# Attention backward on one NeuronCore: score and dP matmuls on four 32-row strips of the array

## The chip, the cores and the metric

The kernel runs on one core of one Trainium2 chip. TensorE (PE in the profile, with PEld for its weight loads) multiplies on an array of 128 rows by 128 columns and writes to PSUM; VectorE (DVE), ScalarE (ACT) and GpSimd (POOL) do the elementwise work; SyncE (SP) issues most DMAs, POOL issues others. The metric is the device time of one execution in microseconds. Three runs of the kernel before took 2552.87 to 2571.11 us, median 2569.79.

A matmul here contracts over the partitions (rows) of its two operands: a stationary one, loaded into the array, and a moving one, whose columns (up to 512) stream through. Where a matmul uses only some rows of the array, its operands lie on the same partitions, and that range of partitions chooses the part of the array.

## The reference

One transformer block with adaptive layer norm, forward and backward. S = 2048 tokens, D = 512, 32 heads of 16 channels, everything handed over in bfloat16. The forward pass returns the output, the backward pass the gradients of the input, the weights and the conditioning vector.

```
h = layernorm(x) * (1 + ca) + sa
x = x + ga * attention(h)          # 32 heads, softmax(q k^T / 4) v, then wo
h = layernorm(x) * (1 + cb) + sb
x = x + gb * mlp(h)                # relu(h w1 + b1)^2 w2 + b2
out, vjp = jax.vjp(f, x, wqkv, wo, w1, b1, w2, b2, c, w_mod);  grads = vjp(grad_out)
```

What the change touches is the attention part of the backward pass. For each head, with P the unnormalised exponentials: scores = q k^T, P = exp(scores / 4), dP = dO v^T minus a term for each query row, dS = P * dP; then dV = P^T dO, dK = dS^T q, dQ = dS k. The kernel folds the normalisation into dO beforehand, and the row term into two extra channels: dO^T has 18 rows a head (16 channels and the row term in two bfloat16 parts), V^T has 18 (16 channels and two rows of ones), so that dP comes out of one matmul over 18 rows. Scores contract over 16 rows.

## The kernel before

The program has three parts: the forward pass with the MLP's backward woven in, the weight gradients of the MLP (`gen_dw1`, `gen_dw2`, from about 1060 to 1179 us), and the attention backward (`attn_bwd`, from 1179 to 2438 us), followed by the projections' gradients (`phase6`).

**Heads and groups.** Four heads form a group g, eight groups in all. In the transposed tensors in DRAM (QTq_d, KTq_d, VTq_d, dOTq_d) each group is 128 partitions by 2048 tokens, and head j of the group takes the 16 or 18 rows from partition 32 j on. For V^T and dO^T the heads are shifted by two places: head j lies from partition 32 ((j + 2) mod 4). The rows between are padding.

**The loop of `attn_bwd`.** For each group, each pair of heads jp (heads 2 jp and 2 jp + 1 of the group), each key chunk c of 512 keys, and each block ib of 128 queries there is one unit: 8 x 2 x 4 x 16 = 1024 units. For each head a of the pair, a unit has a score matmul (L1555, stationary Q^T block, moving K^T chunk, into PSUM tile st), an exponential (ScalarE, L1559, into pu), a dP matmul of the unit before it (L1494, stationary dO^T block, moving V^T chunk, into PSUM tile dp) and VectorE's product of dp and pu into ds (L1496). Every second unit PE also does eight matmuls into acckv (L1448, 16 columns of weights, 512 columns of data, two units' worth), and in the others sixteen into accq (L1470, two units' worth, with 16 columns of data). ds is transposed for accq mostly by DMA, four units at a time; one in eight of its blocks is transposed on PE (L1513) and copied by ScalarE (L1514). st and dp have three PSUM buffers each.

**Masked copies.** A score matmul uses the 64 rows of its pair (partitions 64 jp to 64 jp + 63), a dP matmul the other 64. Both heads' rows of Q^T and dO^T lie there, so the moving operand must be zero on the other head's rows: `self.masked` holds for each of the four heads of a group its own copy of K^T and V^T, each 128 partitions by 2048, in two tiles m01 and m23. They are set to zero once by eight memsets on VectorE (L1375, in `open_bwd`, which is called inside the weight-gradient stage), and after that only the head's own 16 or 18 rows are loaded (`pair_pieces`, L1414).

**Order of the work.** PE's and SyncE's order is that of the program text in all of this; POOL's too from `phase5` on. In the weight-gradient stage VectorE, ScalarE and POOL are still ordered by the scheduler. The loads for the next pair of heads are issued on POOL, spread over the units (L1544), each behind a one-element copy (L1543) that waits for a product of VectorE. m01 is used again at the end: `xhat1_6`, loaded in the last pair, is its first half.

Of the kernel before, what the change touches and what calls it, by code (L numbers as in the profile page):

```python
# [9 lines left out]
BF16 = mybir.dt.bfloat16  # L10
# [9 lines left out]
P = 128  # L20
DH = 16
# [84 lines left out]
class K:  # L106
# [1249 lines left out]
    def open_bwd(self):  # L1356

        nc = self.nc
        S, ST, D, DT = self.S, self.ST, self.D, self.DT
        self.open_pool("pad_r", bufs=1, side="right").tile([P, 240], BF16, name="pad_r")  # L1360
        xp = self.open_pool("p5x", bufs=1, side="right")
        self.wp = self.open_pool("p5w", bufs=1, side="right")
        cp = self.open_pool("p5c", bufs=1, side="right")
        m01 = xp.tile([P, 4 * S], BF16, name="m01")
        self.q0 = xp.tile([P, 2 * S + 3 * ST * 4 * DH], BF16, name="q0")
        self.xhat1_6 = m01[:, :ST * D].rearrange("p (st d) -> p st d", d=D)
        self.wq_6 = self.q0[:, :3 * DT * D].rearrange("p (kt n) -> p kt n", n=3 * D)
        nc.vector.memset(self.kvs[0:64], self.scale)
        nc.vector.memset(self.kvs[64:P], 1.0)
        m23 = cp.tile([P, 4 * S], BF16, name="m23")  # L1370
        self.masked = {n: [m[:, (2 * t + a) * S:(2 * t + a + 1) * S] for m in (m01, m23) for a in range(2)]
                       for t, n in enumerate(("KT", "VT"))}
        for ms in self.masked.values():
            for m in ms:
                nc.vector.memset(m, 0.0)  # L1375
        self.qp = self.open_pool("p5q", bufs=1, side="right")
        self.Tq = {}

# [35 lines left out]
    def pair_pieces(self, g, jp):  # L1414
        pieces = []
        for n, src, sh, rows in (("KT", self.KTq_d, 0, DH), ("VT", self.VTq_d, 2, DH + 2)):
            for j in (2 * jp, 2 * jp + 1):
                r = 32 * ((j + sh) % 4)
                pieces.append((self.masked[n][j][r:r + rows, :], src[g, r:r + rows, :]))
        return pieces  # L1420

    def attn_bwd(self):
# [7 lines left out]
        tc, nc = self.tc, self.nc  # L1430
# [5 lines left out]
        acckv = accp.tile([P, 512], F32, name="acckv")  # L1436
        nc.vector.memset(acckv[:], 0.0)
        accq = accp.tile([P, ST, 2, DH], F32, name="accq")
        masked, kvs = self.masked, self.kvs
        pend, pendq = [], []  # L1440

        def kv(u):
# [46 lines left out]
        def dP(u, a):  # L1489

            (T, g, jp, c, ib, kvT, pu, dsg, i, grp) = u
            rd = slice(64 - 64 * jp, 128 - 64 * jp)
            dp = dpp.tile([P, 512], F32, name="dp")
            nc.tensor.matmul(dp[:], lhsT=T["dOT"][rd, ib * P:(ib + 1) * P],  # L1494
                             rhs=masked["VT"][2 * jp + a][rd, 512 * c:512 * (c + 1)], start=True, stop=True)
            nc.vector.tensor_tensor(dsg[:, i, a], dp[:], pu[:, a, :], ALU.mult)  # L1496

        def dS(u):
# [19 lines left out]
        T = self.T0  # L1518
        turnq, last = [], None
        for g in range(NQ):  # L1520
            for jp in range(2):
# [15 lines left out]
                for c in range(SC):  # L1537
                    c0 = 512 * c
                    for ib0 in range(0, ST, G):
# [6 lines left out]
                        for i in range(G):  # L1546
# [4 lines left out]
                            pu = self.pup.tile([P, 2, 512], BF16, name="pu")  # L1551
                            for a in range(2):
                                stt = stp.tile([P, 512], F32, name="st")
                                rs = slice(64 * jp, 64 * jp + 64)
                                nc.tensor.matmul(stt[:], lhsT=T["QT"][rs, q], rhs=masked["KT"][2 * jp + a][rs, c0:c0 + 512],  # L1555
                                                 start=True, stop=True)
                                if last:
                                    dP(last, a)
                                nc.scalar.activation(pu[:, a, :], stt[:], ACT.Exp, scale=self.scale)  # L1559
# [351 lines left out]
```

The softmax here doesn't subtract the row's maximum and nothing guards it: scores larger than these inputs give would overflow.

## Time and profile before

| | |
|---|---|
| median of three runs | 2569.79 us (2552.87 to 2571.11) |
| span of the profiled execution | 2562.0 us |
| its own time outside the span | not given by the profile |
| PE busy | 2483.2 us, 97% |
| ScalarE busy | 2314.2 us, 90% |
| VectorE busy | 1767.4 us, 69% |
| POOL busy | 569.5 us, 22% |
| mean granted TensorE clock | 0.994 |
| L1496, product of dp and pu, 2048 times | 1236.2 us busy, 13.1 us idle before |
| L1559, exponential, 2048 times | 1073.7 us busy, 46.4 us idle before |
| L1555, score matmul, 2048 times | 638.4 us busy, mean 381 to 382 ns |
| L1494, dP matmul, 2048 times | 690.3 us busy, mean 381 to 382 ns |

How to read it: the page's first lines give the busy time of each engine and its share of the span, then the span in 40 slices. A matmul's line has rows and columns of the array (64*128: 64 rows, 128 columns) and the shape of its operand. Matmuls overlap in the pipeline, so the mean length of one is longer than the time between two starts. A group's busy time counts overlapping instructions once; "idle before" is the time in which the engine stood still just before them, with what ended it. In the tables of stretches each line has the stretch, its length, then busy time and number of instructions for PE, PEld, DVE, ACT and POOL, then the granted clock as a share of full speed, the DMA share and GB/s. In the chain of work each line has start, length and what the end of the program hung on in that time.

### The profile page before, as it was taken

To read this page: it belongs to the slowest core of one execution; us is meant where nothing else is said; L and a number is where in the kernel's file an instruction comes from. 1 tells how busy PE (TensorE), PEld (TensorE's weight loads), DVE (VectorE), ACT (ScalarE), POOL (GpSimd) and SP (SyncE) were. 2 spreads that over 40 slices of the span, in tenths; PEclk is the share of its full clock that TensorE was granted. 3 is DMA by queue.
4 is the path that set the end of the run, shared out by engine and by line. 5 is a ranking of instruction groups with operands and counts; after the bars stand their busy time and mean duration, and the time that the engine had idled before them with its cause. 6 is when DMAs were issued, how large, how long until landed. Compare 5 with 4: busy or idle time off the path is not lost.

```text
span 2562.0 us, 77852 instructions
## 1 busy us (share of the span) xinstructions
PE 2483.2 (97%) x31239; PEld 1227.4 (48%) x31239; DVE 1767.4 (69%) x3651; ACT 2314.2 (90%) x3757; POOL 569.5 (22%) x1137
## 2 busy tenths in 40 slices
PE   8999899999999999899999999999999999999998
PEld 4555555555555554663444444444444444444443
DVE  6222323323322344667999999999999999999957
ACT  7999999999999996436999999999999999999935
POOL 3554521320221131353011111111111111111223
PEclk9999999999999999999999999999999999999999
DMA  4588742450351153799999999999999999999997
GB/s 165 118 180 196 173 95 83 100 113 22 112 128 49 39 143 113 154 190 211 205 205 202 199 200 201 203 204 200 197 199 198 208 201 197 201 201 229 213 202 191
DMA packets 1193040, 425.37 MB, mean 166 GB/s; under 512 B 1138004, under 2 KB 1161686, under 8 KB 1192678
## 3 DMA queue, kind: packets, MB, share of 16 engines
q1 hardware_dynamic: 1153542, 319.25, 64.2%
q0 software_dynamic: 37056, 100.11, 13.1%
q8 instruction: 244, 4.00, 0.6%
q10 hardware_dynamic: 2080, 1.05, 0.1%
q14 instruction: 118, 0.97, 0.1%
HBM read 73.73 MB, written 62.40 MB: 53 GB/s over the span
## 4 chain that ended last, share of the span: by engine, by line
PE 67%; ACT 20%; DMA 5%; issue 4%; POOL 2%; DVE 1%; SPq 1%; POOLq 0%; DVEq 0%; ACTq 0%
PE st L1555 20%; ACT pu L391 16%; PE acckv L1448 11%; PE accq L1470 8%; PE st L388 7%; PE accbank L322 3%; PE dp L1494 3%; ACT pu L1559 2%; PE st L1513 2%; PE dps L1047 2%; PE pps L1234 2%; PE dp L1604 1%; PE st L1699 1%; DMA dsT<-ds 1%; DMA ev_tm<-ev_fm 1%
## 5 line engine op out<-in xcount | busy, mean ns | idle before, releaser
L1496 DVE TENSOR_TENSOR ds<-dp,pu 128x512 bf16<-128x512 f32 x2048 | 1236.2, 679 | 13.1 <-PE dp L1494 10.2
L1559 ACT ACTIVATE pu<-st 128x512 bf16<-128x512 f32 x2048 | 1073.7, 612 | 46.4 <-PE dp L1494 22.5
L391 ACT ACTIVATE pu<-st 128x1024 bf16<-128x1024 f32 x992 | 912.1, 1077 | 4.6 <-PE st L388 4.4
L388 PE MATMUL st<-QTm,KTq 128*128 128x512 bf16 x1984 | 588.6, 377 | 19.5 <-ACT pu L391 6.0
L322 PEld LDWEIGHTS <-pu 128*128 128x128 bf16 x8192 | 347.5, 96 | 236.1 <-issue 3.1
L322 PE MATMUL accbank<-Vaug,pu 128*128 128x17 bf16 x8192 | 357.7, 171 | 1.2 <-ACT Vaug L522 0.9
L1494 PE MATMUL dp<-m,q 64*128 64x512 bf16 x1024 | 345.7, 382 | 1.1 <-DVE g2w L1053 0.7
L1494 PE MATMUL dp<-m,dOTg 64*128 64x512 bf16 x1024 | 344.6, 381 | 0.1
L1470 PEld LDWEIGHTS <-dsT 128*128 128x128 bf16 x8192 | 239.5, 96 | 213.8 <-issue 209.7
L1555 PE MATMUL st<-m,q 64*128 64x512 bf16 x1024 | 319.5, 382 | 9.2 <-ACT pu L1559 7.5
L1555 PE MATMUL st<-m,QTg 64*128 64x512 bf16 x1024 | 318.9, 381 | 9.5 <-ACT pu L1559 7.8
L388 PEld LDWEIGHTS <-KTq 128*128 128x128 bf16 x1984 | 188.3, 96 | 176.9 <-issue 125.5
L1543 POOL COPY tick<-ds 1x1 bf16<-1x1 bf16 x223 | 39.6, 178 | 1005.4 <-DVE ds L1496 1005.4
L1448 PE MATMUL acckv<-ds,q 128*16 128x512 bf16 x1024 | 154.0, 381 | 0.0
L1448 PE MATMUL acckv<-pu,dOg 128*16 128x512 bf16 x1024 | 154.0, 381 | 0.0
L1448 PE MATMUL acckv<-ds,Qg 128*16 128x512 bf16 x1024 | 154.0, 381 | 0.0
L1448 PE MATMUL acckv<-pu,q 128*16 128x512 bf16 x1024 | 154.0, 381 | 0.0
L1514 ACT COPY dsT<-st 128x512 bf16<-128x512 bf16 x256 | 152.4, 595 | 1.0 <-PE st L1513 1.0
L1470 PE MATMUL accq<-Kg,dsT 128*128 128x16 bf16 x4096 | 143.3, 170 | 3.4 <-DMA dsT<-ds 3.4
L1470 PE MATMUL accq<-q,dsT 128*128 128x16 bf16 x4096 | 143.6, 170 | 0.4 <-DMA dsT<-ds 0.3
L302 POOL DMA_DIRECT2D QTm<-QTq_d x124 | 63.3, 512 | 341.3 <-PE st L388 320.2
L329 DVE RECIPROCAL rl<-accbank 128x4 f32<-128x4 f32 x128 | 22.9, 179 | 162.6 <-PE accbank L322 162.5
(379 smaller groups left out, 2864.8 us busy)
## 6 DMA issues: line engine op xcount, KB each, us to landing
KTq<-KTq_d POOLq DMA_DIRECT2D x24, 512.0 KB, 3.9
duT_d<-auT POOLq DMA_DIRECT2D x3, 1792.0 KB, 7.8
aT_d<-rT POOLq DMA_DIRECT2D x3, 1792.0 KB, 11.1
KTq_d<-KTq SPq DMA_DIRECT2D x32, 128.0 KB, 2.0
QTq_d<-ev_fm SPq DMA_DIRECT2D x32, 128.0 KB, 3.9
VTq_d<-vT POOLq DMA_DIRECT2D x4, 1024.0 KB, 6.8
dsT<-ds SPq DMA_TRANSPOSE x256, 6.7
dx<-dx_d SPq DMA_DIRECT2D x16, 256.0 KB, 4.4
```

Source lines behind the costliest of these rows:

```text
L302: nc.gpsimd.dma_start(QTm[j][32 * j:32 * j + 32, :], self.QTq_d[g, 32 * j:32 * j + 32, 512 * qc:512 * (qc + 1)])
L322: nc.tensor.matmul(acc[:, a, sub, :], lhsT=pu[:, a, sub * P:(sub + 1) * P], rhs=Vaug[:, kb, h, :], start=(kb == 0 and a == 0 and sub == 0) ...
L388: nc.tensor.matmul(stt[:, a, :], lhsT=KT[:, kb * P:(kb + 1) * P], rhs=QTm[2 * jp + a][:], start=True, stop=True)
L391: nc.scalar.activation(pu[:], stt[:], ACT.Exp, scale=self.scale)
L1047: nc.tensor.matmul(pt[:], lhsT=a[st], rhs=g_tm[:, st, :], start=(st == 0), stop=(st == ST - 1))
L1448: nc.tensor.matmul(acckv[r:r + DH, :], lhsT=T[n][:, ib, col:col + DH], rhs=src[:, a, :], start=(ib == 0), stop=(ib == ST - 1))
L1470: nc.tensor.matmul(accq[:, ib, a, :], lhsT=dsT[:, (i * 2 + a) * 4 + sub, :], rhs=T["K"][:, 4 * c + sub, col:col + DH], start=(c == 0 and i ...
L1494: nc.tensor.matmul(dp[:], lhsT=T["dOT"][rd, ib * P:(ib + 1) * P], rhs=masked["VT"][2 * jp + a][rd, 512 * c:512 * (c + 1)], start=True, sto ...
L1496: nc.vector.tensor_tensor(dsg[:, i, a], dp[:], pu[:, a, :], ALU.mult)
L1514: nc.scalar.copy(dsT[:, 0:4, :], tp[:])
L1555: nc.tensor.matmul(stt[:], lhsT=T["QT"][rs, q], rhs=masked["KT"][2 * jp + a][rs, c0:c0 + 512], start=True, stop=True)
L1559: nc.scalar.activation(pu[:, a, :], stt[:], ACT.Exp, scale=self.scale)
```

## The change

`open_bwd` no longer makes m23 and the masked copies: there are two tiles, KTg and VTg, each 128 partitions by 2048, for the four heads of a group together, and no memsets. m01 stays, for `xhat1_6` alone. `pair_pieces` loads the same rows as before, into these two tiles. The score matmul contracts over the 16 rows of its own head (r = 32 (2 jp + a)), the dP matmul over the 18 of its own (r = 32 ((2 jp + a + 2) mod 4)), so that the four matmuls of a unit lie on four different 32-row strips of the array. Moving columns, outputs, order and number of the matmuls stay as they were; the eight memsets are the only instructions that go.

```diff
@@ open_bwd
-        m23 = cp.tile([P, 4 * S], BF16, name="m23")
-        self.masked = {n: [m[:, (2 * t + a) * S:(2 * t + a + 1) * S] for m in (m01, m23) for a in range(2)]
-                       for t, n in enumerate(("KT", "VT"))}
-        for ms in self.masked.values():
-            for m in ms:
-                nc.vector.memset(m, 0.0)
+        self.kvT = {n: cp.tile([P, S], BF16, name=n) for n in ("KTg", "VTg")}
@@ pair_pieces
-                pieces.append((self.masked[n][j][r:r + rows, :], src[g, r:r + rows, :]))
+                pieces.append((self.kvT[n + "g"][r:r + rows, :], src[g, r:r + rows, :]))
@@ attn_bwd
-        masked, kvs = self.masked, self.kvs
+        KTg, VTg, kvs = self.kvT["KTg"], self.kvT["VTg"], self.kvs
@@ dP
-            rd = slice(64 - 64 * jp, 128 - 64 * jp)
+            r = 32 * ((2 * jp + a + 2) % 4)
-            nc.tensor.matmul(dp[:], lhsT=T["dOT"][rd, ib * P:(ib + 1) * P],
-                             rhs=masked["VT"][2 * jp + a][rd, 512 * c:512 * (c + 1)], start=True, stop=True)
+            nc.tensor.matmul(dp[:], lhsT=T["dOT"][r:r + DH + 2, ib * P:(ib + 1) * P],
+                             rhs=VTg[r:r + DH + 2, 512 * c:512 * (c + 1)], start=True, stop=True)
@@ the score matmul
-                                rs = slice(64 * jp, 64 * jp + 64)
-                                nc.tensor.matmul(stt[:], lhsT=T["QT"][rs, q], rhs=masked["KT"][2 * jp + a][rs, c0:c0 + 512],
+                                r = 32 * (2 * jp + a)
+                                nc.tensor.matmul(stt[:], lhsT=T["QT"][r:r + DH, q], rhs=KTg[r:r + DH, c0:c0 + 512],
                                                  start=True, stop=True)
```

## The prediction

> **What bounds the kernel now.** I read the page's head and slices first, to find the stage that the change touches, then the table of stretches for that stage, its groups, and the chain of work.
>
> ```profile
> span 2562.0 us, 77852 instructions
> PE 2483.2 (97%) x31239; PEld 1227.4 (48%) x31239; DVE 1767.4 (69%) x3651; ACT 2314.2 (90%) x3757; POOL 569.5 (22%) x1137
> PEclk9999999999999999999999999999999999999999
> ...
> 1600.00:1700.00 100.00, 98.54 (x1412) 42.49 (x1409) 99.22 (x166) 97.81 (x195) 11.83 (x34) 1.00 1.06 204
> 1800.00:1900.00 100.00, 98.35 (x1403) 42.67 (x1404) 98.43 (x164) 97.34 (x196) 12.10 (x35) 1.00 1.02 201
> ```
>
> Score and dP matmuls (L1555, L1494) exist only in the attention backward, from the first exponential at 1179.0 us to the last product at 2437.7: 1258.7 us for 1024 units (a unit is one pair of heads, one key chunk, one query block), 1.229 us each. In its stretches PE is 98% busy, VectorE 98 to 99%, ScalarE 97%. The page's average (VectorE 69%) hides that VectorE is full here. The groups from 1600 to 2200 us:
>
> ```profile
> L1496 DVE TENSOR_TENSOR ds<-dp,pu 128x512 bf16<-128x512 f32 x980 | 591.4, 678 | 5.9 <-PE dp L1494 4.5 <-issue 0.4
> L1559 ACT ACTIVATE pu<-st 128x512 bf16<-128x512 f32 x980 | 513.5, 612 | 11.6 <-PE dp L1494 10.5
> L1494 PE MATMUL dp<-m,dOTg 64*128 64x512 bf16 x512 | 172.3, 381 | 0.0
> L1555 PE MATMUL st<-m,QTg 64*128 64x512 bf16 x512 | 159.3, 381 | 4.6 <-ACT pu L1559 3.8
> ```
>
> VectorE spends 591.4/980 = 0.603 us on a product, two a unit: 1.207 us, and it was idle 5.9 of 600 us. So VectorE is the floor, and PE waits for it inside the dP matmuls. How PE's own unit is made up stands in the chain of work:
>
> ```profile
> 1800.66 0.54 PE acckv L1448 x8
> 1801.20 0.32 PE st L1555
> 1801.52 0.00 PE dp L1494
> 1801.52 0.21 PE st L1555
> 1801.73 0.05 PE dp L1494
> 1801.78 0.49 PE accq L1470 x16
> 1802.28 0.32 PE st L1555
> ```
>
> A score and a dP matmul lie in different halves of the array and run together: a round of 512 columns is 0.21 us, and the first round after another kind of work 0.32, 0.11 more. Two rounds a unit, 0.53 us. Every second unit has eight acckv matmuls (0.54), the others sixteen accq (0.49); four transposes come every fourth (0.24), a few at the end of a pair (about 0.02 a unit). PE alone: 0.53 + 0.27 + 0.245 + 0.06 + 0.02 = 1.13 us of the 1.23.
>
> **The change part by part.** *Strips.* The four matmuls of a unit now lie on four different strips, so two rounds can become one: 0.53 to 0.32 us, PE's unit to 0.92. If the strips did not overlap, nothing changes. But PE is not the floor: at 0.603 us, 2048 products and 15 L1477 instructions of 0.68 us need 1246 of the 1257 us in which VectorE has such work. Hidden behind VectorE, the 0.21 us are worth at most 11 us, at least nothing; I take 11 at full clock. Stored shapes, numbers of instructions and DMAs stay.
>
> *Loads.* In the built program every K and V load waits for the same count of PE as before, though the four heads now share two tiles; only the first moves four places up POOL's queue. The rest costs nothing: the loads are issued a pair ahead. The loads of xhat1 into m01 in the last pair lose a wait on PE that was over by then.
>
> *Memsets.* Eight of 0.912 us on VectorE go (L1375, from 1069.5 us). They lie in the weight-gradient stage, where PE then starved:
>
> ```profile
> 1069.53 0.91 DVE L1375 MEMSET m<- 128x1024 uint32 x1 [3.73 <-DMA dOTq_d<-dOTq]
> 1072.85 0.79 POOL L1014 DMA_DIRECT2D out_dram<-dw  x1 [4.00 <-DVE junk L1011]
> 1080.14 0.35 DVE L1006 SCALAR_TENSOR_TENSOR dw<-dps,opcbT,t 128x128 bf16<-128x128 f32 x1 [3.99 <-DMA out_dram<-dw]
> 1084.14 1.44 PE L992 MATMUL dps<-tm_blk,xh 128*128 128x128 bf16 x12 [6.85 <-DVE junk L1008]
> ```
>
> The first memset held VectorE for the dOTq store until 1069.5; that delayed the store of 1072.85, whose landing released VectorE at 1080.1; two more memsets (2.1 us with their issue) stood before PE's release. The first K load now carries the dOTq wait on POOL; queued behind it are that store of 1072.85 and the next weight block's load (L972). So the store leaves at about 1069.4, 3.4 us earlier. That is up to 5.5 us, and 2.8 more if the half clock of 1084.1 to 1089.8 goes; nothing, if the later stall of 3.72 us at 1118.66, behind another store, takes it back. I take 5, bounds 0 and 9.
>
> *What the array does in between.* The same stretch of time with fewer rows at work can cost the clock. Stretches of 3.41 us on the grid on which the granted clock changes (busy PE, ..., clock, DMA, GB/s):
>
> ```profile
> 1069.31:1072.72 3.41, 2.07 (x35) 1.90 (x32) 3.03 (x13) 0.00 (x0) 0.00 (x0) 1.00 1.17 234
> 1072.72:1076.13 3.41, 2.85 (x52) 2.85 (x52) 3.08 (x14) 1.53 (x6) 3.10 (x4) 1.00 1.16 187
> 1178.53:1181.95 3.42, 2.32 (x15) 0.76 (x14) 3.06 (x6) 2.92 (x6) 1.84 (x2) 1.00 0.09 38
> 1181.95:1185.36 3.41, 3.41 (x16) 1.03 (x13) 3.41 (x6) 3.21 (x8) 0.00 (x0) 0.50 0.01 2
> ```
>
> With 2.07 us busy the clock stayed; with 2.32 us, at the start of our stage, it halved. The difference is height: the first window has 128-row matmuls (about 30 of 128 columns, 0.053 us each: 1.6 us, 0.47 of it), the second ten 64-row matmuls of 0.213 us. Count those half: 1.07 us and three transposes, 1.23 us, 0.36. The half-clock window after it has twelve 64-row matmuls, 12 x 0.107 = 1.28 us, 0.38, and the clock comes back; one at 1082.96 has 22 of 128x128, 0.34, and it does not. Sorted so, every window of this trace fits one threshold between 0.36 and 0.39 of full height; sorted by time streamed, they do not (that window streams 0.51, others stay full at 0.47). This is inference from one trace.
>
> [...]
>
> A unit of our stage in that count, before: scores and dP 4 x 0.213 x 1/2 = 0.427; accq 8 x 16 columns and one transpose a unit 0.053 each; acckv 4 x 0.213, full height but 16 columns wide: whole 0.853, as a 32-column quarter 0.213, as 16/128 0.107. Over 1.229 us: 1.13, 0.61 or 0.52, all above 0.39. After: scores and dP 0.213 (a strip is 32 of 128) or 0.113 (16 and 18 rows as such). The trace cannot tell which count holds:
> - columns ignored: 0.95 or 0.87; clock stays full.
> - rows and columns by 32: 0.532/1.229 = 0.43, scattering (by 0.04 if I reweigh the windows of this trace) about the threshold.
> - real rows, real columns, or one of them: 0.27, 0.35, 0.35; clock lost, and as the stage starts at half clock, not regained.
>
> *Price of the half clock.* Rounds double, 0.427 us; the 0.11 I leave, since after the transposes of 1181.94, already at half clock, it was about 0.12. Narrow matmuls keep their pace: nine of 17 columns begun 0.16 us before the clock returned took 0.42 us, nine at full clock 0.38. Strips 0.54; acckv (2 x 0.427 + 0.11)/2 = 0.48; accq 0.26; transposes (4 x 0.107 + 0.11)/4 = 0.13; rest 0.02. Together 1.43 us a unit, above VectorE's 1.207: PE becomes the floor. 1024 x 1.43 = 1464 instead of 1259: +205 us. Bounds: 0, if all still hid behind VectorE; +605, if all of PE's 0.92 doubled (1.84 us). I take 1.43, whose rows are measured at half clock, and 1.40 to 1.53 for its own spread.
>
> Sum for the forecast: 2562 + 205 - 5 = 2762; I say **2762**. The span of the profiled execution lies 8 us under the median of the three runs (2569.79; 2552.87 to 2571.11), and its own time outside the span is not shown; my sum is on the span, so the comparison may be off by that.
>
> **Rivals.**
> 1. *The clock stays; faster.* One mechanism: the gate ignores columns, PE sheds 0.21 us a unit and VectorE runs without gaps. For it: full clock through all the stage, 11 us of idle VectorE. Against: VectorE is full. 2562 - 11 - 5 = 2546 (2535 to 2556). It decides if full-height work stays over 0.39.
> 2. *The clock flickers.* Counted by 32, warm windows stand at 0.43 and half-clock ones at 0.532/1.43 = 0.37: it falls and returns. With 10 to 40% of units at half clock, 20 to 80 us: 2566 to 2626.
> 3. *Strips don't run four at a time.* Then two rounds remain, 2557, unless the clock goes too.
>
> **How the numbers follow.** Half clock through the stage 0.46; flicker 0.22 (half of it over +1%); full clock 0.30; no overlap 0.02. 1%, 26 us, is about what runs of this kernel tell from none. Faster by more: the lower third of the full-clock case, 0.11. Slower: 0.46 + 0.11 + 0.02 = 0.59. Within: 0.30. Range: 2535, the full-clock case's low end, to 2865, where 1.53 us a unit ends (2562 + 308 - 5). It is wide because the cases are far apart; the forecast's own is 2732 (1.40 us) to 2865.
>
> **What would show it.** Right: granted clock at 0.5 to 0.6 from 1180 us on, VectorE near 85% there, its idle time ended by dP, 512-column matmuls of about 0.6 us instead of 0.38. Wrong: clock at 1.00 and VectorE still 99%: then the gate does not weigh columns. Four starts within 0.05 us show the strips; no PE wait at 1084 shows the memsets' part. A unit of over 1.6 us at half clock would mean that the drains or narrow matmuls double too.

## The result

The changed kernel takes 2917.28 us, the median of four runs (2917.0 to 2921.27); the kernel before, run beside it, 2563.68 (2552.87 to 2571.11). The ratio is 1.139, with a 95% interval of 1.136 to 1.143: 353 us slower. The prediction said slower, by the clock, and 2762; the time lies 52 us above its range.

The head of the profile of the kernel after and its row of granted clock (40 equal slices of the span, here 73 us each, in tenths of full speed):

```profile
span 2915.2 us, 77844 instructions
...
PE 2870.1 (98%) x31239; PEld 1253.9 (43%) x31239; DVE 1819.6 (62%) x3643; ACT 2355.3 (81%) x3757; POOL 568.9 (20%) x1137
...
PEclk9999999999999999555555555555555555555589
```

The clock is full for sixteen slices and half for the next twenty-two. Its events put the fall at 1163.2 us and the return at 2798.2: 1635 us without a break. The execution with the profile took 2917.13 us, so 1.9 lie outside the span.

The table of stretches of the kernel after (stretch, length, busy PE, PEld, DVE, ACT, POOL with instructions, clock, DMA share, GB/s): three on the grid of the clock at the start of the stage (in the traces of before and after, the changes of the granted clock lie whole multiples of 3.413 us apart: 339, 479 and 33 in after), and two of those shown of before:

```profile
1159.83:1163.24 3.41, 2.31 (x15) 0.75 (x16) 3.23 (x6) 3.21 (x7) 1.84 (x2) 1.00 0.10 38
1163.24:1166.65 3.41, 3.33 (x17) 0.81 (x15) 3.41 (x7) 3.06 (x7) 0.10 (x1) 0.50 0.00 0
1166.65:1170.06 3.41, 3.27 (x24) 0.86 (x20) 2.59 (x5) 2.56 (x5) 0.60 (x2) 0.50 1.05 241
...
1600.00:1700.00 100.00, 100.00 (x1081) 34.65 (x1080) 79.67 (x128) 77.21 (x149) 9.69 (x28) 0.50 0.74 155
1800.00:1900.00 100.00, 100.00 (x1088) 34.98 (x1085) 79.68 (x127) 77.83 (x150) 8.95 (x26) 0.50 0.76 155
```

The clock falls in the first window of strips, at almost the same busy time (2.31 us) that cost the kernel before one window at its own start. There it came back after 3.4 us; here it does not. In the stage PE is busy all of the time (100.00 of 100 us) and VectorE 80%: the floor has passed from VectorE to PE. The groups from 1600 to 2200 us show it from VectorE's side; the first line answers the product line of before (5.9 us idle, 980 products):

```profile
L1491 DVE TENSOR_TENSOR ds<-dp,pu 128x512 bf16<-128x512 f32 x752 | 475.8, 684 | 122.3 <-PE dp L1489 80.1 <-ACT dsT L1509 19.8 <-ACT dv_t L1458 17.4
L1554 ACT ACTIVATE pu<-st 128x512 bf16<-128x512 f32 x751 | 405.4, 595 | 116.9 <-PE dp L1489 105.0 <-PE st L1550 11.9
L1489 PE MATMUL dp<-VTg,q 18*128 18x512 bf16 x471 | 181.3, 601 | 0.0
...
L1443 PE MATMUL acckv<-pu,q 128*16 128x512 bf16 x480 | 122.9, 614 | 0.0
```

From stage to stage: the first exponential comes at 1159.4 us, 19.6 earlier than the 1179.0 of before (1.6 of that was there before 1050 us; how much of the rest is scatter stands under the memsets). The attention backward then takes 1635.0 us to its last product at 2794.4, against 1258.7: +376.3, or 1.597 us a unit for 1.229. What follows takes 120.8 for 124.3. 2562.0 - 19.6 + 376.3 - 3.5 = 2915.2.

### The profile page after: what moved, and what is told of

It is laid out like the page before. It is cut to its first block, busy times and chain, and to the rows that moved or that the text cites. A ratio compares the mean times of both kernels' runs of the same rounds, so it can differ in the third digit from the quotient of the medians.

```text
span 2915.2 us, 77844 instructions
## 1 busy us (share of the span) xinstructions
PE 2870.1 (98%) x31239; PEld 1253.9 (43%) x31239; DVE 1819.6 (62%) x3643; ACT 2355.3 (81%) x3757; POOL 568.9 (20%) x1137
## 4 chain that ended last, share of the span: by engine, by line
PE 79%; ACT 15%; issue 2%; DMA 2%; POOL 1%; DVE 1%; SPq 0%; ACTq 0%; POOLq 0%; DVEq 0%
PE st L1550 23%; PE acckv L1443 17%; ACT pu L391 14%; PE accq L1465 9%; PE st L388 7%; PE st L1508 4%; PE accbank L322 3%; PE dp L1489 2%; PE dps L992 1%; PE dps L1047 1%; PE dp L1599 1%; PE pps L1234 1%; PE st L1694 1%; PE st L1454 1%; PE pps L631 1%
## 5 line engine op out<-in xcount | busy, mean ns | idle before, releaser
L1491 DVE TENSOR_TENSOR ds<-dp,pu 128x512 bf16<-128x512 f32 x2048 | 1295.4, 684 | 330.2 <-PE dp L1489 218.9
L1489 PE MATMUL dp<-VTg,q 18*128 18x512 bf16 x1024 | 394.7, 599 | 1.3 <-DVE g2w L1053 0.9
L1489 PE MATMUL dp<-VTg,dOTg 18*128 18x512 bf16 x1024 | 394.6, 601 | 0.0
L1550 PE MATMUL st<-KTg,q 16*128 16x512 bf16 x1024 | 367.0, 596 | 0.6 <-ACT pu L1554 0.3
L1550 PE MATMUL st<-KTg,QTg 16*128 16x512 bf16 x1024 | 366.6, 598 | 0.0
L1443 PE MATMUL acckv<-pu,q 128*16 128x512 bf16 x1024 | 262.3, 614 | 0.0
L1443 PE MATMUL acckv<-ds,q 128*16 128x512 bf16 x1024 | 262.3, 614 | 0.0
L1443 PE MATMUL acckv<-pu,dOg 128*16 128x512 bf16 x1024 | 262.3, 614 | 0.0
L1443 PE MATMUL acckv<-ds,Qg 128*16 128x512 bf16 x1024 | 262.3, 614 | 0.0
L1550 PEld LDWEIGHTS <-q 16*128 16x128 bf16 x1024 | 54.1, 98 | 235.0 <-issue 231.8
```

Source lines behind the costliest of these rows:

```text
L1443: nc.tensor.matmul(acckv[r:r + DH, :], lhsT=T[n][:, ib, col:col + DH], rhs=src[:, a, :], start=(ib == 0), stop=(ib == ST - 1))
L1489: nc.tensor.matmul(dp[:], lhsT=T["dOT"][r:r + DH + 2, ib * P:(ib + 1) * P], rhs=VTg[r:r + DH + 2, 512 * c:512 * (c + 1)], start=True, stop ...
L1550: nc.tensor.matmul(stt[:], lhsT=T["QT"][r:r + DH, q], rhs=KTg[r:r + DH, c0:c0 + 512], start=True, stop=True)
```

## The experiments

The theory was that the clock costs the time, and that the granted clock follows how many rows of the array are at work (what grants it is the gate of the prediction and of the expectations; the traces show the granted clock alone). Four questions were open. Is it the clock alone? Is the clock lost by the start of the stage or by its steady mix? Which count of the work does the clock follow? And why is a unit at half clock 1.60 us and not 1.43?

### The clock alone

*fill_wide* keeps the array at work with matmuls that nobody needs: 128 rows, 128 columns of weights, written where the score matmul writes next. There are two of 512 columns per score in the first eight units, one per score in the next eight, then 1280 columns in every two units. *fill_narrow* is the same with 16 columns of weights.

```diff
+                                for w in ([512] * (2 if n < 8 else 1) if n < 16 else [] if a else [512, 256] if i % 2 else [512]):
+                                    nc.tensor.matmul(stt[0:128, 0:w], lhsT=self.ones_b[:, 0:128], rhs=T["QT"][:, c0:c0 + w],
+                                                     start=True, stop=True)
```

> The changed kernel with filler matmuls of 128 rows by 128 columns ahead of the score matmuls, into the tile that the score then overwrites: 1280 columns in two units, 0.267 us of PE a unit at full clock (more in the first 16 units, so that the stage doesn't start at half clock). Work that nobody needs, added. If the clock follows rows times columns at work, the count rises to (0.326 + 0.267) / 1.21 = 0.49 and the clock is 1.00: PE's unit is 0.92 + 0.27 = 1.19 us, VectorE is the floor again, the stage about 1255 us and the span about 2545. If the four strips lose time in themselves, the clock stays half, a unit is 1.60 + 0.53 us and the span about 3460.

> The same fillers with 16 columns of weights instead of 128, so that rows, columns streamed and PE's busy time are those of the wide fillers and only the width differs. If the gate counts the width of the array at work, the count is (0.326 + 0.033) / 1.21 = 0.30 and the clock is half: a unit of 1.60 us plus most of 0.53, span 3290 to 3460 us. [...]

fill_wide: 2654.88 us, ratio 1.039 (1.036 to 1.041), clock 1.00 through the whole stage. fill_narrow: 2677.47 in its one run, clock 1.00 in the stage too. With work added, the kernel is some 250 us faster than without it. That is the clock, and nothing in the strips themselves. The chain of work of fill_wide (start, length, what):

```profile
1801.15 0.54 PE acckv L1443 x8
1801.69 0.32 PE st L1551
1802.01 0.32 PE st L1554
1802.33 0.00 PE dp L1489
1802.33 0.01 PE st L1554
1802.34 0.07 PE dp L1489
1802.41 0.49 PE accq L1465 x16
```

At full clock the four strips need 0.32 us together where two rounds needed 0.53: they do run four at a time. Both times lie above the 2545 that fill_wide was expected to take at full clock, because the needless work is on the path: 0.21 us and one more change between kinds of work, 0.11, in each block. In fill_narrow the matmul behind acckv costs 0.21 only; it and acckv both take 128 rows by 16 columns.

The clock was 1.00 in both, with weight blocks of 16 columns as with blocks of 128: counted by real columns (0.30), fill_narrow was expected at half clock. So in these two runs the clock did not follow the number of weight columns.

### Start or steady mix

*warm_start* keeps only the needless matmuls of the first 16 units (`for w in [512] * (2 if n < 8 else 1 if n < 16 else 0)`).

> The kernel after, with needless 128-row matmuls (128x128 weights of ones, 512 columns, result overwritten by the score matmul) ahead of the scores of the first 16 units only: two per score in units 0 to 7, one in units 8 to 15. They add about 16 x 0.4 + 8 x 0.4 = 10 us at most. It asks whether after's steady mix of work holds the clock once it has it. Theory 'real rows' (a strip of 16 or 18 rows counts 16 or 18 of 128): a warm unit of 1.21 us counts 0.43/1.21 = 0.35 to 0.36 of full height, under the 0.36 to 0.39 that the kernel before showed, so the clock falls soon after the fillers end: 2917 to 2930 us, granted clock 0.50 from about 1200 on. Rival 'strips of 32' (a strip counts 32 rows whatever lies in it): 0.53/1.21 = 0.44, the clock holds and after only lost it at the stage's start: 2535 to 2560 us, granted clock 1.00 nearly throughout.

2920.7 us, ratio 1.139 (1.133 to 1.145). The clock stayed full until 1199.2 us, after the last of the added work (1191.7), then fell and was half for 1607.7 us. The start is not the cause; the steady mix loses the clock.

### What the clock follows: the rows

*warm_rows32* lets the same matmuls contract over the 32 rows of their strip, padding included; *warm_both32* also widens acckv's weights from 16 to 32 columns.

```diff
-        for n, src, sh, rows in (("KT", self.KTq_d, 0, DH), ("VT", self.VTq_d, 2, DH + 2)):
+        for n, src, sh, rows in (("KT", self.KTq_d, 0, 32), ("VT", self.VTq_d, 2, 32)):
-            nc.tensor.matmul(dp[:], lhsT=T["dOT"][r:r + DH + 2, ib * P:(ib + 1) * P],
+            nc.tensor.matmul(dp[:], lhsT=T["dOT"][r:r + 32, ib * P:(ib + 1) * P],
-                                nc.tensor.matmul(stt[:], lhsT=T["QT"][r:r + DH, q], rhs=KTg[r:r + DH, c0:c0 + 512],
+                                nc.tensor.matmul(stt[:], lhsT=T["QT"][r:r + 32, q], rhs=KTg[r:r + 32, c0:c0 + 512],
```

> warm_start, and the score and dP matmuls contract over all 32 rows of their strip; the rows beyond 16 or 18 are the zero padding of the tensors in DRAM, which is loaded with the rest, so the sums are the same and no matmul takes longer. Theory 'real rows': a warm unit now counts 0.53/1.21 = 0.44, the clock holds through the stage: 2535 to 2560 us, faster than or the same as before, granted clock 1.00, VectorE 98% busy in the stage. Rival 'strips of 32': the same as warm_start, whichever way that goes. Rival 'only values that change count' (rows of zeros do no work): the same as warm_start at half clock, 2917 to 2930.

> warm_rows32, and the acckv matmuls with 32 columns of weights where they had 16 (the other pair's columns too, whose results are not read). If the width of weights counts by real columns, this adds 0.107 us to a unit's count (0.35 to 0.44 of full height): full clock here and half clock in warm_rows32. If the width does not count, as the fillers of 16 columns suggest, it goes as warm_rows32 goes, within 0.5%.

warm_rows32 took 2712 to 2872 us in four runs (median 2805.68), each with another share of half clock; warm_both32 took 2796.09 in its one run, within that spread, so it decides nothing. The slices of granted clock in warm_rows32, in the fastest of its four runs:

```profile
PEclk9999999999999999996999965899955569555589
```

Nothing but rows of zeros was added, no matmul takes longer (at full clock a mean of 381 to 382 ns on 32 rows in rows32_fill, 381 to 384 on 16 and 18 in fill_narrow), and the clock now comes and goes: half for 705 of the 1428 us of the stage in that run, in stretches of 17 to 277 us. It came back more than once within the stage, so half clock did not lock in; but it was not held, and the 2535 to 2560 expected were wrong. 32 rows for 16 and 18 took the steady mix from half clock throughout (warm_start, from 1199.2 us on) to one that comes and goes. Where the clock is full, from 1300 to 1560 us, a unit takes 1.224 us. That is what the strips are worth at full clock against the 1.229 of before: some 6 us in 1024 units.

*kv3_rows32_warm*, *kv3_rows32* and *kv3_warm* were to add full-height time without an instruction, by an order of a block's eight acckv matmuls that asks for the same columns of the array again before the other columns have begun.

```diff
+            order = [(0, 0), (0, 1), (1, 0), (0, 2), (0, 3), (1, 1), (1, 2), (1, 3)]
+            for k, s in order if len(us) == 2 else [(0, 0), (0, 1), (0, 2), (0, 3)]:
```

> warm_rows32, whose clock went up and down, with the same eight acckv matmuls of a block in another order, so that they need three rounds of the array where they had two (a column of the array is asked for again before its neighbours have begun): full-height work for 0.213 us more in two units, and no instruction more. Theory 'the gate counts rows at work and the time they stream': the warm unit goes from about 0.53/1.21 = 0.44 of full height to 0.64/1.21 = 0.53, well clear of the threshold, and PE's unit is 0.92 + 0.11 = 1.03 to 1.15 us, still under VectorE's 1.21: granted clock 1.00 through the stage, no run of the slower kind, 2535 to 2555 us, faster than before by 0.3 to 1.1%. Rival 'the flicker has another cause (heat, power, the start)': it goes on, 2650 to 2870 us.

> kv3_rows32_warm without the needless matmuls at the start: only the 32 rows and the order of the acckv matmuls differ from the kernel after. The stage starts at half clock, as in after. By the count, half-clock windows now hold 0.37 to 0.40 of full height, up to 0.45 at times, so a window soon passes the threshold and the clock comes back within about 100 us and then stays: 2540 to 2590 us. Rival 'half clock locks in': it stays at half for most of the stage, with a unit of 1.6 to 1.75 us: 2800 to 3080 us.

> kv3_rows32_warm with the 16 and 18 rows of the kernel after: the order of the acckv matmuls and the needless matmuls at the start are the only differences from after. By the count a warm unit is (0.113 + 0.32 + 0.106)/1.21 = 0.445 of full height, as in warm_rows32: if rows and time alone count, it flickers as that kernel did, 2650 to 2880 us, mean clock 0.75 to 0.90. Rival 'only the strips' height matters': half clock from about 1200 on, and a unit of 1.7 to 1.8 us with the longer acckv block: 3000 to 3130.

The edit did nothing to the time in the array. The timeline of kv3_rows32 at full clock:

```profile
1401.73 0.39 PE L1445 MATMUL acckv<-ds,Qg 128*16 128x512 bf16 x2
1401.74 0.39 PE L1445 MATMUL acckv<-pu,dOg 128*16 128x512 bf16 x2
1401.94 0.38 PE L1445 MATMUL acckv<-ds,Qg 128*16 128x512 bf16 x2
1401.95 0.38 PE L1445 MATMUL acckv<-pu,dOg 128*16 128x512 bf16 x2
```

The program's third matmul is a ds one on the columns of the first. The two pu matmuls that follow it in the program began with the first two, within 0.01 us, and the third 0.21 us later: still two rounds. So these kernels are repeats of the ones without the order, and their expectations can't be judged. kv3_rows32_warm ran from 2657 to 2936 us in eight runs (median 2775.31), the up and down of warm_rows32; in the slowest of the eight, which has the profile, the clock was half for 1603 of the stage's 1639 us, and in the fastest, by its mean clock of 0.916, for about 446 us (an estimate: 2 x 0.084 of its 2654.9). kv3_rows32, which has no needless work at all, took 2810.46 (2802 to 2819), with half clock for 1167 of 1528 us. So in these runs with 32 rows the clock was full for anything from two thirds of the stage down to almost nothing. kv3_warm, with 16 and 18 rows, took 2924.59, as the kernel after. In the profiles of all five kernels with 16 or 18 rows and no steady added work (after, warm_start, kv3_warm, and memsets_back and half_width below), the stage was at half clock, once the added work had ended, but for 0 to 17 us.

### What the clock follows: full-height time

*rows32_fill* adds full-height time in a way that was measured to take it (0.21 us a matmul in fill_narrow): warm_rows32 with narrow needless matmuls at the start, and after that one of 512 columns in every second unit, straight behind acckv. The others vary it: 768 columns (*rows32_fill768*), 16 and 18 rows (*rows16_fill*), nothing at the start (*rows32_fill_cold*), and one in every fourth unit with nothing at the start (*rows32_fill4*).

```diff
+                                for w in ([512] * (2 if n < 8 else 1) if n < 16 else [512] if not a and not i % 2 else []):
+                                    nc.tensor.matmul(stt[0:16, 0:w], lhsT=self.ones_b[:, 0:16], rhs=T["QT"][:, c0:c0 + w],
+                                                     start=True, stop=True)
```

> Scores and dP over the 32 rows of their strip, needless matmuls (128 rows, 16 columns of weights) in the first 16 units as in warm_rows32, and then one of 512 columns in every second unit, straight behind the acckv block, where the kernel with fillers of 16 columns showed 0.21 us for one. It is what the new order of the acckv block was to give and did not (its eight matmuls still went through in two rounds). Theory 'rows at work x time': a warm unit goes from 0.53/1.21 = 0.44 of full height, where the clock went up and down, to 0.64/1.21 = 0.53; PE's unit is 0.92 + 0.11 + waits, under VectorE's 1.21: granted clock 1.00 through the stage, 2535 to 2565 us, faster than before or the same. Rival 'the flicker has another cause': clock 0.72 to 0.92, 2650 to 2950.

> rows32_fill with 768 columns of needless work in every second unit where it has 512: 0.05 us a unit more for PE, 0.69/1.25 = 0.55 of full height. Theory: clock 1.00 here too; VectorE still sets the pace or PE is just above it: 2540 to 2600 us. If 0.53 is not enough and rows32_fill flickers, this one does so less.

> rows32_fill with the 16 and 18 rows of the kernel after. By the count a warm unit holds (0.432 + 0.107)/1.21 = 0.445 of full height, as much as warm_rows32, whose clock went up and down. Theory 'rows at work x time, whoever does the work': it flickers too, 2600 to 2900 us, clock 0.75 to 0.97. Rival 'a strip's 32 rows count whole': 0.53, clock 1.00, 2535 to 2565. Rival 'fillers count for nothing': as after, 2917 and more.

> rows32_fill without the needless matmuls of the first 16 units, so that the stage starts at half clock. A half-clock unit holds (0.532 + 0.107)/1.65 = 0.39 of full height, at the threshold, with windows above it: the clock comes back within 20 to 150 us and then stays, 2540 to 2600 us. Rival 'half clock locks in': most of the stage at half, 2850 to 3050.

> rows32_fill_cold with one needless matmul of 512 columns in every fourth unit in place of every second; no needless work at the start. It asks where, between 0.44 (goes up and down) and 0.53 (holds) of full height, the clock begins to hold, and whether the strips at full clock can be as fast as the kernel before. 0.485 by the count. Theory: PE's needless work falls from 0.107 to 0.053 us a unit, and the unit from 1.286 towards the 1.217 of warm_rows32 at full clock, to 1.24 to 1.26: with the clock held 2555 to 2580 us, the same as before. Rival: 0.485 is not enough, the clock goes up and down with 0.80 to 0.97 mean: 2600 to 2800.

Measured, slower than expected where the clock held, but for rows32_fill4, which lies at the end of its range: rows32_fill 2610.36 us, ratio 1.017 (1.015 to 1.020). rows32_fill768 2658.87, ratio 1.037 (1.033 to 1.041). rows16_fill 3081.55, ratio 1.201 (1.195 to 1.208). rows32_fill_cold 2604.66, ratio 1.016 (1.011 to 1.020). rows32_fill4 2577.88, ratio 1.006 (1.003 to 1.009). The slices of clock of rows32_fill, then of rows16_fill, then of rows32_fill4:

```profile
PEclk9999999999999999999999999999999999999999
```

```profile
PEclk9999999999999999555555555555665785555579
```

```profile
PEclk9999999999999999995999999999999999999999
```

The pair that shows the rows by themselves is rows16_fill and rows32_fill: the same instructions in the same order and with the same columns, and only the rows of the strips (and of their loads) differ, by rows of zeros. The first had a mean clock of 0.74 and 0.73 in its two runs, the second 0.997 to 0.999 in its five.

In one count these runs stand in order. The count is height at work (16, 18, 32, 64 or 128 rows of 128) times the time that columns stream at full clock, four strips together counting their rows, two rounds of acckv counting 0.427 us whatever their width. That 512 columns count 0.213 us and 128 columns 0.053 is the author's estimate, from the 0.21 us of a round in the chain of before; in its trace the two rounds of acckv start 0.219 us apart and the transposes 0.055. Strips then give a unit 0.113 us of full height (16 and 18 rows) or 0.213 (32), acckv 0.213, accq 0.053, transposes 0.053, a needless 512 columns 0.213. Divided by the unit at full clock:

| kernel | full height per unit, us | unit at full clock, us | share | clock in the stage (profiled run) |
|---|---|---|---|---|
| after | 0.432 | 1.21 (VectorE's floor) | 0.36 | half throughout |
| rows16_fill | 0.539 | 1.286 | 0.42 | half; full for 197 of 1784 us, 57 of them at the start |
| warm_rows32 | 0.532 | 1.224 | 0.43 | up and down, half for 705 of 1428 us; in kv3_rows32_warm, with the same count, 1603 of 1639 |
| rows32_fill4 | 0.585 | 1.245 | 0.47 | half for 68 us at the start, then full but for two windows of 3.4 us |
| rows32_fill | 0.639 | 1.278 | 0.50 | full throughout |
| rows32_fill768, fill_narrow, fill_wide | 0.692, 0.699, 0.699 | 1.325, 1.347, 1.324 | 0.52 to 0.53 | full throughout |
| before | 0.746 | 1.230 | 0.61 | full but for a first window |

In these runs the clock was never kept at 0.36, kept for part of the time at 0.42 and 0.43, and always from 0.50 on, whether the rows belong to needless matmuls or to zeros in a strip. rows16_fill was expected to go up and down at 0.445; its unit was longer than assumed, which makes it 0.42, and it was nearly always at half clock, with a unit of 1.81 us there.

These are averages, and in the traces the clock changes between windows of 3.41 us. Counted in the same way for every window of all 19 profiles (15219 windows; columns at half clock count the same, though they take longer: most transposes start 0.106 to 0.107 us apart there in after), one threshold fits best: the clock in the next window was full above 0.377 of full height and half below, with 33 exceptions, 30 of them between 0.36 and 0.39. The best threshold of a count that leaves out the rows, time streamed alone, has 95 exceptions, among them 31 of the 73 falls of the clock, where the count by rows has 1; with rows rounded up to 32 it has 141. So the 0.36 to 0.39 that the prediction read from before fits these 19 profiles too. The averages that held the clock are higher, and the lowest windows show why: with a mean of 0.45 at full clock, warm_rows32 has windows down to 0.36.

| kernel, windows of the stage | at full clock: mean, lowest | at half clock: mean, highest |
|---|---|---|
| after | none | 0.28, 0.375 |
| warm_rows32 | 0.45, 0.36 | 0.34, 0.41 |
| rows32_fill4 | 0.48, 0.36 | 0.35, 0.40 |
| rows32_fill | 0.51, 0.43 | none |
| before, from 1186 us on | 0.62, 0.505 | none |

rows32_fill_cold settles the start: at half clock from 1162.9 us, it is back at 1197.0 and stays. But none of these beats the kernel before. What the needless work costs (1.278 and 1.245 us a unit for 1.224) is more than the 6 us that the strips are worth.

### Why 1.60 us and not 1.43

*half_width* is the kernel after with the exponential and the product over 256 columns where there were 512. It leaves out half of the exponentials and products, so its time is not one of the whole work; PE's instructions are the same.

```diff
-            nc.vector.tensor_tensor(dsg[:, i, a], dp[:], pu[:, a, :], ALU.mult)
+            nc.vector.tensor_tensor(dsg[:, i, a].bitcast(F32), dp[:, 0:256], pu[:, a, :].bitcast(F32), ALU.is_ge)
-                                nc.scalar.activation(pu[:, a, :], stt[:], ACT.Exp, scale=self.scale)
+                                nc.scalar.activation(pu[:, a, :].bitcast(F32), stt[:, 0:256], ACT.Exp, scale=0.0)
```

> The kernel after, with ScalarE's exponential and VectorE's product over 256 columns where they had 512: this leaves out half of the exponentials and products, so its time is no time of the whole work. PE's instructions are the same ones. It asks why a unit at half clock takes 1.60 us and not the 1.43 of the sum. Theory: with three PSUM buffers the second pair of strips waits for an exponential and a product of the unit before; with these cut to about half, the four strips start together in all units, the unit falls to 1.40 to 1.47 us, the stage to 1434 to 1505 and the span to 2715 to 2790, still at half clock. Rival: the strips after accq are late for a reason of PE's own (draining, weight loads): the unit stays at 1.57 to 1.60 us, the span at 2885 to 2915.

Its span is 2787.1 us, within what the theory expected, and from 1200 to 1900 us, at half clock without a break, a unit takes 1.464 us in place of 1.598. First the timeline of the kernel after, two units:

```profile
1802.45 0.60 PE L1550 MATMUL st<-KTg,QTg 16*128 16x512 bf16 x1
1802.45 0.60 PE L1489 MATMUL dp<-VTg,dOTg 18*128 18x512 bf16 x1
1802.45 0.60 PE L1550 MATMUL st<-KTg,QTg 16*128 16x512 bf16 x1
1802.46 0.60 PE L1489 MATMUL dp<-VTg,dOTg 18*128 18x512 bf16 x1
1802.99 0.60 PE L1465 MATMUL accq<-Kg,dsT 128*128 128x16 bf16 x16
1803.52 0.60 PE L1550 MATMUL st<-KTg,QTg 16*128 16x512 bf16 x1
1803.53 0.60 PE L1489 MATMUL dp<-VTg,dOTg 18*128 18x512 bf16 x1
1803.79 0.58 PE L1550 MATMUL st<-KTg,QTg 16*128 16x512 bf16 x1
1803.94 0.58 PE L1489 MATMUL dp<-VTg,dOTg 18*128 18x512 bf16 x1
1804.45 0.60 PE L1443 MATMUL acckv<-ds,Qg 128*16 128x512 bf16 x2
```

Behind acckv all four start within 0.01 us. Behind accq the second head's pair is late, by 0.27 and 0.41 us, and everything after it too. Three PSUM buffers hold one and a half units: the second score of a unit writes where ScalarE is still reading the unit before (its exponential ends about 1803.74), the second dP where VectorE is (about 1803.89). acckv takes 0.96 us, long enough for both to finish; accq, 0.53, is not. Now the chain of work of half_width:

```profile
1802.65 0.96 PE acckv L1443 x6
1803.61 0.53 PE st L1550
1804.15 0.01 PE dp L1489 x2
1804.16 0.53 PE accq L1465 x16
1804.69 0.54 PE st L1550
1805.22 0.13 PE dp L1489 x2
1805.35 0.96 PE acckv L1443 x6
```

Behind transposes the second pair is no longer late; behind accq the second dP still is, by less. By the starts of PE's blocks, the time from the first strip to the next kind of work is 0.712 us a unit in the kernel after (0.56 behind acckv, 0.93 behind accq, 0.77 behind transposes) and 0.582 in half_width. acckv gives 0.481 and 0.480, accq and transposes together 0.407 and 0.402: unchanged. The wait for the buffers is shown; the experiment takes away 0.13 us a unit of it. What is left behind accq looks like the same wait: from 1200 to 1900 us the second dP of a block straight behind accq is late by 0.42 us on average in the kernel after and by 0.15 in half_width, and every one of them (110 and 120) begins 0.05 us after the end of a product of VectorE. In one unit of four, 0.15 us is 0.04 a unit; this part is read from the traces, and no run took it away.

### The memsets

*memsets_back* puts eight memsets into the kernel after, at the old place (on m01 and the two new tiles). *late_memsets* is the kernel before with its memsets behind `fill.until("half")` in the program text. *pool_memsets* is the kernel before with its memsets on GpSimd:

```diff
         for ms in self.masked.values():
             for m in ms:
-                nc.vector.memset(m, 0.0)
+                nc.gpsimd.memset(m, 0.0)
```

> The changed kernel with eight memsets of the old size on VectorE at the old place (four on m01, two each on KTg and VTg), so that only this part of the change is undone. If the memsets and the store that they wait for are what brought the weight-gradient stage's end from 1178.7 to 1159.1 us, the attention backward starts at about 1178 us again and the span is 2915 + 18 = 2933 us. If the earlier start came from the freed tiles or the moved K load, it stays at 1159 and 2915. The clock in the attention backward is half in both cases.

> The kernel before, with its eight memsets moved down in the program behind the first half of the second weight gradient, so that they no longer stand in VectorE's queue while the first weight gradient needs it. Masked copies and 64-row matmuls stay. If the memsets' place cost the 18 us, the attention backward starts at about 1160 us and the span is 2562 - 18 = 2544 us at full clock; if what freed time in the changed kernel was the tiles, it stays at 2562.

> The kernel before, with its eight memsets on GpSimd where they stood on VectorE; nothing else. It does the memsets' part of the change alone on the old kernel. The kernel after, against the one with the memsets put back, began the attention backward 12.5 us earlier. Theory 'VectorE's queue': the memsets cost what they do because VectorE stands behind the first of them until a store has landed; on GpSimd they leave PE's waits of 1.8 and 6.1 us and the half clock of 1084 to 1090 away: the stage starts at 1165 to 1172 in place of 1179 to 1180, 2545 to 2555 us, faster than before by 0.3 to 0.6%. Rival 'the store': GpSimd issues the weight gradient's stores itself, and the store of 1072.85 then stands behind the waiting memset: the delay stays, 2558 to 2570.

memsets_back: 2925.91 us, ratio 1.1445 (1.141 to 1.148). Its stage starts 12.5 us later than that of after (1171.9 for 1159.4 us), with the old waits back, as its timeline of PE shows (in brackets, the idle time and what ended it):

```profile
1071.62 0.83 PE L992 MATMUL dps<-tm_blk,xh 128*128 128x128 bf16 x12 [1.84 <-DVE junk L1008]
...
1081.72 1.44 PE L992 MATMUL dps<-tm_blk,xh 128*128 128x128 bf16 x12 [6.09 <-DVE junk L1008]
...
1091.54 0.83 PE L992 MATMUL dps<-tm_blk,xh 128*128 128x128 bf16 x12 [0.69 <-DVE junk L1008]
```

The kernel after has one such wait between 1060 and 1125 us, of 0.99 us. Single profiles scatter here, though. Up to this stage, after and its variants without memsets do the same work, and their first exponential comes from 1159.4 (after itself, the earliest) to 1166.6 us in fourteen profiles, and at 1174.0 in the fifteenth, half_width, with one wait of 11.67 us; with the memsets on VectorE it comes at 1171.9, 1173.2 (late_memsets) and 1179.0 (before, the latest). By medians that is 10 us.

late_memsets moved nothing: 2558.91 us, ratio 1.0007 (0.9991 to 1.0023). The scheduler, which orders VectorE in this stage, put the first memset back to where it stood, waiting 3.58 us for the same store:

```profile
1068.07 0.91 DVE L929 MEMSET m<- 128x1024 uint32 x1 [3.58 <-DMA dOTq_d<-dOTq]
```

pool_memsets takes 2551.26 us (2546.97 to 2566.49, 13 runs), ratio 0.9965 (0.9953 to 0.9976): 0.35% faster than the kernel before, and so than both kernels of this study. That is 7.9 us by the medians, 6 to 12 by the interval, and the best measure of what the memsets' place on VectorE cost. Its weight-gradient stage, in the profiled run, has PE waits of 1.43, 0.39, 0.44 and 1.96 us and one window of half clock, and its attention backward starts at 1166.6, 12.4 us before the kernel before does. (That run is the longest of the thirteen; it loses time behind the stage again.) The same work costs less where no one stands behind it: GpSimd spends 14.2 us on the eight memsets, where VectorE spent 7.3, and VectorE's longest wait for a store beside them is 3.03 us, where it was 3.99. How much of the cost was VectorE's wait at the first memset (3.73 us) and how much the clearing is not shown, since both leave VectorE here.

## Why the prediction was right or wrong

**What bounds the kernel, and that PE would take over: right.** VectorE was the floor, and it went from 98 to 80% busy, idle mostly for PE's dP (80.1 of 122.3 us from 1600 to 2200). The forecast said about 85%, for its shorter unit.

**The clock: right, and its rivals wrong.** Half from the first window of the stage, 512-column matmuls of 0.60 us, never regained. It was given a chance of 0.46, since the trace of before could not choose between the counts; which one holds, the runs above had to show. The threshold read from that trace, 0.36 to 0.39, fits all the profiles (0.377, with 33 exceptions in 15219 windows). Of the three counts, "columns ignored" is refuted for the way it was used: it gave acckv 0.853 us, one for each matmul, although four of them run at a time. Its 1.13 of full height for the kernel before, more than the whole array, was a sign of that. Counted by rounds, columns can be ignored and the count is 0.36, with real rows, as in the third bullet. "By 32", which made the flicker, fits a kernel that was not asked about: it is what 32 real rows in a strip do, and there the up and down costs 95 to 375 us over the kernel before (2657 to 2936), not 20 to 80.

Busy time does not sort these kernels: from 1600 to 1700 us PE was busy 100.00% in after with the clock at 0.50, and 100.00% in fill_wide and 98.07% in rows32_fill with the clock at 1.00.

**The price of the half clock: the step that failed.** The sum of 1.43 us a unit was made of strips 0.54, acckv 0.48, accq 0.26, transposes 0.13 and rest 0.02. Measured: strips 0.712, acckv 0.481, accq, transposes and rest 0.407 (forecast 0.41). All but the strips held to 0.005 us. Strips were priced as four at a time in every unit; at half clock they are that only behind acckv. 0.17 us too little, times 1024, is 174 us, against the 171 by which the stage came out longer than forecast (376 for 205). half_width takes 0.13 of it away; the other 0.04 is there even so, and by its traces is the rest of the same wait behind accq. The bound of 1.53 was too low for the same reason: it spread the measured rows, and left out that a new wait, for the readers of PSUM, could stand in PE's order once ScalarE and VectorE were no longer the floor but not far from it either. The sign of "over 1.6 us" was missed by a hair (1.597) and would have misled: accq grew only from 0.49 to 0.53 us, and nothing but the strips was off. The upper bound of +605 us is a slip: 1.84 us a unit makes +625.

**The memsets: right in mechanism, somewhat too small.** Forecast 5 us, bounds 0 and 9. Measured 8 us in time, with the memsets on GpSimd (6 to 12), and about 10 at the start of the stage by the medians of the profiles; the 12.5 and 12.4 of single pairs lie within the scatter around that. The later wait that the forecast feared would take the gain back, 3.72 us at 1118.66 in the kernel before, went as well in the profile of after (nothing over 1 us there).

**The strips' gain at full clock: right in sign, half the size.** At most 11 us was the sum; 1.224 for 1.229 us a unit makes 6.

**Sum.** -5 became -19.6 at the start of the stage, +205 became +376.3, and the tail, not forecast, gave -3.5. The -19.6 is luck of the two profiles in part, the latest start against the earliest. The two errors have opposite signs; the strips' term is the one that put the time outside.

## What to carry to other kernels

Before narrowing matmuls to fewer rows, work out how much of each window of 3.41 us the array is at full height, not only how busy PE is: here windows under 0.377 were followed by half clock and those over it by full, but for 33 of 15219, so that an average of 0.36 lost it for a whole stage, 0.43 kept it for part of the stage, by chance, and 0.50 held it throughout; the half clock cost some 350 us, the strips were worth 6. When an engine becomes slower than its neighbours by little, price its waits for their buffers unit by unit, not its instructions alone: here they were 0.17 us of 1.60 a unit. A memset that waits for a store belongs on an engine whose queue nobody needs (8 us here, by pool_memsets), and its place in that queue is read in the trace, not in the program text (late_memsets).

## What the runs showed of the hardware

- Rows at work and the clock: strips of 16 and 18 rows were at half clock for 1635 us with PE busy throughout (after). With a needless matmul in every second unit, 16 and 18 rows were at half clock for 1587 of 1784 us (rows16_fill), and the same instructions with rows of zeros added at full clock throughout (rows32_fill).
- Windows and the clock: in windows of 3.41 us, counted by rows at work times time, the clock of the next window was full over 0.377 of full height and half below, in all but 33 of 15219 windows of the 19 profiles of this case.
- Weight columns and the clock: with needless matmuls of 128 rows by 16 columns the clock was 1.00 in the stage (fill_narrow, rows32_fill), as with 128 by 128 (fill_wide).
- Order of starts: in kv3_rows32 the third of eight acckv matmuls of the program, on the same columns of the array as the first, began at 1401.94 us, 0.20 after the fourth and fifth, on other columns (1401.74), and the eight took two rounds, 0.54 us.
- Weight columns and time: behind acckv (128 rows by 16 columns), a needless matmul of 512 columns took 0.32 us with 128 columns of weights (fill_wide) and 0.21 with 16 (fill_narrow).
